# Attention over a KV cache on one core: four kv heads to a unit instead of two

## The chip, the cores and the metric

One core of one Trainium2 chip. The metric is the device time of one execution in microseconds (us); times of several executions are given as their median. Some executions are over 1.5% above the fastest of the same kernel and are called slow; comparisons use the others, the fast ones. A profiled execution gives a span, which is some 1.8 us shorter than the execution's time.

The terms: PE is the engine of the matrix products, DVE and ACT are those of element-wise work and copies. HBM is the chip's main memory, SBUF the core's working memory, PSUM the memory that takes PE's results. A load *lands* when its last bytes and its semaphore have arrived. The *granted clock* is the share of PE's full clock that PE was given.

## The reference

```python
B, Sq, D = 8, 4, 512;  Hq, Hkv, Sk, Dh = 32, 8, 2048, 128      # all bf16
q = (x @ wq) as [B, Hq, Sq, Dh]
scores = q . k * Dh**-0.5        # each of the 8 kv heads serves 4 query heads
o = softmax(scores) . v
out = o as [B, Sq, Hq*Dh] @ wo   # [8, 4, 512]
```

K and V are 33.6 MB each, wq and wo 4.2 MB each: 75.5 MB have to be read from HBM.

## The kernel before

It works through 32 units of two kv heads of one batch. A unit's K (1 MiB) lies on 128 partitions in rows of 8 KiB. PE transposes K (as pairs of bf16 in fp32) into PSUM, DVE copies that to SBUF, PE makes scores from it, ACT takes their exponentials, PE transposes the probabilities, ACT copies them to SBUF (block by block, between zeros), and PE multiplies them with V. The units are interleaved by hand; each engine runs its instructions in the order of this program.

```python
KB, VB = 7, 6                                   # K and V buffers of 1 MiB
def load_k(u):
    ...
    nc.sync.dma_start(ks[u][:, :, :],
        k_cache[b, 2*p : 2*p + 2].rearrange("g (s c) d -> (g s) c d", c=C))

def scores(u):
    s_ps = psum_s.tile([128, JT, 2, 64], FP32, tag="s", name="s_ps")   # 2 KiB
    for g in range(2):
        for e in range(2):
            for t in range(4):
                nc.tensor.matmul(s_ps[t*32:(t+1)*32, :, g, :], lhsT=q_bd[...],
                                 rhs=kt[(u, t)][:, :, g*64:(g+1)*64, e], ...)
    ...
    for g in range(2):                          # after the matmuls of both
        nc.scalar.activation(out=s_sb[:, :, g, :], in_=s_ps[:, :, g, :], func=EXP, ...)

def probs_to_keys(u):
    ...                                         # 4 transposes of 128x128 into pt
    for g in range(2):
        rows = slice(g*64, (g+1)*64)
        nc.scalar.copy(out=pr[rows, :, g, :], in_=pt[rows, :, :]...)   # 64 x 512

for n in range(NU + A):                         # w = n - 2
    transpose_part(n, 0); transpose_part(n, 1)
    scores(n - 1)
    transpose_part(n, 2); transpose_part(n, 3)
    values(w); norms(w) if w % 2 == 0; finish(w)     # guards cut
    probs_to_keys(n - 1)
    load_ready(...)                             # issues loads whose buffer comes free
```

The first 480 rows of wo go to SBUF in eight loads of five partitions each, the rest of wo in loads of 128 partitions.

The softmax here doesn't subtract the row's maximum and nothing guards it: scores larger than these inputs give would overflow.

## Time and profile before

| | before |
|---|---|
| time, median of 3 | 191.22 us (189.67 to 192.31) |
| span of the profiled execution | 188.2 us |
| busy: PE, DVE, ACT | 149.1, 109.0, 69.4 us |
| mean granted clock of PE | 0.945 |
| read from HBM | 75.5 MB |

The prediction below shows the views that carry the argument.

### The profile page before, as it was taken

To read this page: it belongs to the slowest core of one execution; us is meant where nothing else is said; L and a number is where in the kernel's file an instruction comes from. 1 tells how busy PE (TensorE), PEld (TensorE's weight loads), DVE (VectorE), ACT (ScalarE), POOL (GpSimd) and SP (SyncE) were. 2 spreads that over 40 slices of the span, in tenths; PEclk is the share of its full clock that TensorE was granted. 3 is DMA by queue.
4 is the path that set the end of the run, shared out by engine and by line. 5 is a ranking of instruction groups with operands and counts; after the bars stand their busy time and mean duration, and the time that the engine had idled before them with its cause. 6 is when DMAs were issued, how large, how long until landed. Compare 5 with 4: busy or idle time off the path is not lost.

```text
span 188.2 us, 5654 instructions
## 1 busy us (share of the span) xinstructions
PE 149.1 (79%) x2483; PEld 123.5 (66%) x2483; DVE 109.0 (58%) x217; ACT 69.4 (37%) x202; POOL 6.3 (3%) x9
## 2 busy tenths in 40 slices
PE   0535799978788788899999988787799888888493
PEld 0515488857676567788877767676588677667372
DVE  0580598765467577447876756657376767663220
ACT  2001574461343334144455352524245433436200
POOL 8400000000000000000000000000000000000000
PEclk9999999999699999858999999999699999999958
DMA  6999999999999999999999999999999999999960
GB/s 212 456 446 383 426 432 417 428 428 429 417 427 423 425 421 434 420 421 432 427 416 428 430 416 428 427 421 421 428 423 423 428 421 423 427 427 413 384 239 8
DMA packets 10952, 75.92 MB, mean 403 GB/s; under 512 B 1288, under 2 KB 1416, under 8 KB 2568
## 3 DMA queue, kind: packets, MB, share of 16 engines
q1 hardware_dynamic: 10880, 75.55, 96.0%
q8 instruction: 19, 0.31, 0.6%
q14 instruction: 5, 0.04, 0.1%
q10 hardware_dynamic: 48, 0.02, 0.0%
HBM read 75.53 MB, written 0.03 MB: 402 GB/s over the span
## 4 chain that ended last, share of the span: by engine, by line
DMA 76%; PE 17%; DVE 2%; issue 1%; ACT 1%; SPq 0%
DMA k_sb<-in_k_cache_dram 50%; DMA v_sb<-in_v_cache_dram 10%; DMA wo_m<-in_wo_dram 9%; DMA x_sb<-in_x_dram 7%; PE kp L198 6%; PE out_ps L397 3%; PE s_ps L261 2%; PE psq L220 2%; DVE kt L200 1%; PE o_ps L321 1%; PE l_ps L303 1%; DVE q_bd L245 1%; PE pt L280 1%; PE nat L345 0%; PE pse L236 0%
## 5 line engine op out<-in xcount | busy, mean ns | idle before, releaser
L200 DVE COPY kt<-kp 128x1024 bf16<-128x1024 bf16 x128 | 82.7, 686 | 38.5 <-PE kp L198 38.5
L198 PE MATMUL kp<-ident,k_sb 128*128 128x128 f32 x512 | 74.6, 293 | 22.6 <-DMA k_sb<-in_k_cache_dram 13.4
L198 PEld LDWEIGHTS kp<-ident,k_sb 128*128 128x128 f32 x512 | 59.7, 149 | 34.4 <-issue 16.2
L286 ACT COPY probs<-pt 64x512 bf16<-64x512 bf16 x64 | 37.1, 579 | 54.2 <-PE pt L280 53.8
L272 ACT ACTIVATE s_sb<-s_ps 128x256 bf16<-128x256 f32 x64 | 23.9, 379 | 33.4 <-PE s_ps L261 19.5
L321 PE MATMUL o_ps<-probs,v_sb 128*128 128x32 bf16 x1024 | 30.7, 177 | 1.2 <-ACT probs L286 0.7
L321 PEld LDWEIGHTS <-v_sb 128*128 128x128 bf16 x1024 | 30.0, 96 | 2.4 <-DMA v_sb<-in_v_cache_dram 1.7
L261 PE MATMUL s_ps<-kt,q_bd 128*32 128x256 bf16 x512 | 21.7, 291 | 0.0
L261 PEld LDWEIGHTS <-q_bd 128*32 128x32 bf16 x512 | 10.9, 97 | 6.7 <-issue 5.7
L311 DVE RECIPROCAL r_sb<-l_ps 128x64 f32<-128x64 f32 x16 | 8.9, 558 | 8.8 <-PE l_ps L303 8.8
L272 ACT ACTIVATION_READ_ACCUMULATOR s_sb<-s_ps 128x1 f32 x64 | 12.7, 198 | 0.0
L280 PE MATMUL pt<-ident,s_sb 128*128 128x128 bf16 x128 | 12.6, 221 | 0.0
L303 PE MATMUL l_ps<-by_gq,ones 128*128 128x64 f32 x32 | 7.2, 307 | 5.5 <-DVE by_gq L296 5.5
L303 PEld LDWEIGHTS l_ps<-by_gq,ones 128*128 128x128 f32 x32 | 5.0, 195 | 7.1 <-DVE by_gq L296 5.3
L280 PEld LDWEIGHTS <-s_sb 128*128 128x128 bf16 x128 | 9.1, 106 | 0.2 <-ACT s_sb L272 0.2
L332 DVE TENSOR_TENSOR oT<-o_ps,r_sb 128x32 bf16<-128x32 f32 x32 | 6.1, 191 | 4.7 <-PE o_ps L321 4.0
L227 ACT ACTIVATE qT_all<-psq 128x256 bf16<-128x256 f32 x4 | 1.5, 383 | 16.8 <-PE psq L220 16.8
L397 PE MATMUL out_ps<-wo_sb,oP 128*32 128x256 bf16 x48 | 5.5, 404 | 0.0
L245 DVE CAST q_bd<-pse 64x512 bf16<-64x512 f32 x4 | 2.6, 681 | 4.6 <-PE pse L236 4.6
L173 POOL MEMSET wo_e<- 64x6144 bf16 x1 | 5.2, 5211 | 0.3 <-POOLq L470 0.3
L296 DVE TENSOR_TENSOR by_gq<-l_sb,by_q 128x64 f32<-128x64 f32 x16 | 3.4, 215 | 2.1 <-ACT s_sb L272 2.1
L397 PEld LDWEIGHTS <-oP 128*32 128x32 bf16 x48 | 3.7, 142 | 1.1
(45 smaller groups left out, 38.0 us busy)
## 6 DMA issues: line engine op xcount, KB each, us to landing
k_sb<-in_k_cache_dram SPq DMA_DIRECT2D x32, 1024.0 KB, 19.6
v_sb<-in_v_cache_dram SPq DMA_DIRECT2D x32, 1024.0 KB, 13.1
wq_sb<-in_wq_dram SPq DMA_DIRECT2D x1, 4096.0 KB
wo_sb<-in_wo_dram SPq DMA_DIRECT2D x4, 512.0 KB
wo_sb<-in_wo_dram SPq DMA_DIRECT2D x4, 256.0 KB, 7.9
wo_m<-in_wo_dram SPq DMA_DIRECT2D x1, 512.0 KB
wo_e<-in_wo_dram SPq DMA_DIRECT2D x8, 60.0 KB
x_sb<-in_x_dram SPq DMA_DIRECT2D x1, 32.0 KB, 14.1
```

Source lines behind the costliest of these rows:

```text
L173: nc.gpsimd.memset(wo_e[:, :, :], 0.0)
L198: nc.tensor.transpose(kp[:, j, :], k4[:, w : w + 128], ident4[:, :])
L200: nc.vector.tensor_copy(out=k_t[:, :, :, :].rearrange("k j s e -> k (j s e)"), in_=kp[:, :, :].rearrange("k j s -> k (j s)").bitcast(BF16),)
L261: nc.tensor.matmul(s_ps[t * 32 : (t + 1) * 32, :, g, :], lhsT=q_bd[:, p, e, b, g, :, :], rhs=kt[(u, t)][:, :, g * 64 : (g + 1) * 64, e], s ...
L272: nc.scalar.activation(out=s_sb[:, :, g, :], in_=s_ps[:, :, g, :], func=EXP, accum_out=l_sbs[u][:, u % 2, g : g + 1])
L280: nc.tensor.transpose(pt[:, j, :], s_sbs[u][:, j, :, :].rearrange("q g s -> q (g s)"), ident[:, :])
L286: nc.scalar.copy(out=pr[rows, :, g, :], in_=pt[rows, :, :].rearrange("s j (c q) -> s (j c) q", q=HQ),)
L303: nc.tensor.matmul(l_ps[:, :, :].rearrange("d u q -> d (u q)"), lhsT=ones[:, :], rhs=by_gq[:, :, :, :].rearrange("k u g q -> k (u g q)"), ...
L311: nc.vector.reciprocal(r_sb[:, :, :], l_ps[:, :, :])
L321: nc.tensor.matmul(o_ps[:, :], lhsT=vs[u][:, 2 * (t * JT + j) + c, :], rhs=pr[:, i, :, :].rearrange("s g q -> s (g q)"), start=(i == 0), s ...
L332: nc.vector.tensor_tensor(out=oT[(p + 1) // 2][:, :, (p == 2) * 1, b, :], in0=o_pss[u][:, :].rearrange("d (h s) -> d h s", h=HP), in1=r_sb ...
L397: nc.tensor.matmul(out_ps[half * T : (half + 1) * T, :], lhsT=o, rhs=w[:, half * DH : (half + 1) * DH], start=(p == 0 and r == 0), stop=(p ...
```

## The change

The intent: K and V in units of four heads, so that each row on a partition is 16 KiB and each transfer 2 MiB; fewer, longer packets for the same bytes. There are then 16 units, 3 + 3 buffers of 2 MiB, and 320 wo rows go through five engines. The compute is rearranged to fit. The core of the diff:

```diff
-    KB = 7
-    VB = 6
+    KB = 3
+    VB = 3
-    NE, WE, WM = 40, 12, 4
+    NE, WE, WM, WN = 40, 8, 5, 64
-            k_cache[b, 2 * p : 2 * p + 2].rearrange("g (s c) d -> (g s) c d", c=C),
+        rows = cache[b, 4 * p : 4 * p + 4].rearrange("g (s c) d -> (g s) c d", c=C)
 ...                                                    (ktpool 6 -> 5, psum_s 1 -> 2)
-        s_ps = psum_s.tile([128, JT, 2, 64], FP32, tag="s", name="s_ps")
-        for g in range(2):
+        for g2 in range(2):
+            s_ps = psum_s.tile([128, 2, JT, 32], FP32, tag="s", name="s_ps")
+            for g1 in range(2):
+                g = 2 * g2 + g1
 ...                                                    (the 8 matmuls of group g)
-        for g in range(2):
-            nc.scalar.activation(
-                out=s_sb[:, :, g, :], in_=s_ps[:, :, g, :], func=EXP, ...
+                nc.scalar.activation(
+                    out=s_sb[:, :, g, :], in_=s_ps[:, g1, :, :], func=EXP, ...
 ...
-        for g in range(2):
-            rows = slice(g * 64, (g + 1) * 64)
+        for g in range(4):
+            rows = slice(g * 32, (g + 1) * 32)
             nc.scalar.copy(                             (64 x 512 -> 32 x 1024)
 ...
-        for t in range(2):
-            if 0 < n < NU:
-                transpose_part(n, t)
+        if 0 < n < NU:
+            transpose_part(n, 0)
         if 0 <= n - 1 < NU:
             scores(n - 1)
-        for t in range(2, 4):
+        for t in range(1, 4):
 ...                                                    (norms each unit; ends cut)
```

## The prediction

> **What bounds the kernel now.** I read the page's slices first, then the busy time by stretch, then the DMA queue's own waits, then the chain and the timeline of the end. The slices (one digit or number for each fortieth of the span, 4.7 us):
>
> ```profile
> PE   0535799978788788899999988787799888888493
> DMA  6999999999999999999999999999999999999960
> GB/s 212 456 446 383 426 432 417 428 428 429 417 427 423 425 421 434 420 421 432 427 416 428 430 416 428 427 421 421 428 423 423 428 421 423 427 427 413 384 239 8
> ```
>
> The 16 DMA engines are busy in every slice from the second to the last but two, at one rate, while PE has gaps everywhere. The busy time by stretch (start:end; then PE, PE weight load, DVE, ACT, POOL busy us; granted clock, DMA share, GB/s) gives the rate in the middle and its fall at the end:
>
> ```profile
> 80.00:100.00 20.00, 19.43 (x304) 16.53 (x308) 13.81 (x27) 9.15 (x26) 0.00 (x0) 0.86 1.01 424
> 100.00:120.00 20.00, 17.87 (x316) 14.51 (x305) 13.06 (x26) 8.50 (x27) 0.00 (x0) 1.00 1.01 424
> ...
> 178.00:180.00 2.00, 1.72 (x25) 1.47 (x21) 0.60 (x2) 0.00 (x0) 0.00 (x0) 0.50 0.88 343
> 180.00:181.00 1.00, 1.00 (x13) 0.63 (x12) 0.27 (x1) 0.00 (x0) 0.00 (x0) 0.50 0.83 326
> 181.00:182.00 1.00, 1.00 (x13) 0.71 (x14) 0.29 (x1) 0.00 (x0) 0.00 (x0) 0.50 0.57 217
> 182.00:183.00 1.00, 1.00 (x12) 0.76 (x10) 0.00 (x0) 0.00 (x0) 0.00 (x0) 0.50 0.37 143
> ```
>
> In the middle: share 1.01 and 424 GB/s, nothing idle. From 178 us the engines run dry one after another. The DMA queue's own waits show that it is held back by transfers still in flight, hardly by compute freeing a buffer:
>
> ```profile
> SPq L123 <- DMA v_sb<-in_v_cache_dram: 47.4, 22, 2.9
> SPq L113 <- DMA k_sb<-in_k_cache_dram: 44.2, 22, 2.2
> ...
> SPq L123 <- PE kp L198: 4.7, 15, 0.4
> ```
>
> The last stretch of the chain of waits (start, us, what) shows how the end hangs on the last landings:
>
> ```profile
> 160.13 16.31 DMA wo_m<-in_wo_dram
> 176.44 0.04 issue
> 176.48 0.82 PE out_ps L397 x10
> 177.31 0.94 PE o_ps L321 x32
> ...
> 181.01 4.11 PE out_ps L397 x40
> 185.13 0.02 issue
> 185.15 0.37 ACT out_sb L453
> ```
>
> So the time is: a start of 2.4 us until bytes flow, a solid stream of 75.5 MB, and some 9 us of dependent work after wo_m lands at 176.48, which runs beside the last 3 MiB of wo.
>
> **One packet.** The trace's record of DMA packets (start, duration, size) has median durations of 84 ns for 2 KiB, 159 for 4 KiB, 309 for 8 KiB, 460 for 12 KiB and 1213 for 32 KiB (the rows of wq). They lie on a line: (1213 - 309) / 24,576 B = 36.8 ps per byte, which is 435 GB/s on 16 engines, plus 8 ns. On one engine the next packet starts 3 ns before the last one ends, so an 8 KiB packet takes 306 ns of an engine, and a semaphore packet (9 ns) takes 6. The fixed part is therefore only some 5 ns in 306.
>
> **What the Trainium skill says.**
> "DMA: Bandwidth & Descriptors", section "Bandwidth", measures 341 GB/s for one transfer of 1 MB and 425 for 16 MB and advises large transfers. That is for a transfer by itself. This trace has 1 MiB transfers at 424 GB/s, since up to eight are queued: the fixed cost is already hidden, and 2 MiB can't win it again.
> The same page, "Why small descriptors are slow (HBM only)", gives a fixed cost of about 3 cycles per packet. The trace agrees that there is a small fixed part: 5 ns in 306.
> The same page, "Why a DMA increments its semaphore by 16 and not by 1", says that a load of 5 partitions uses 5 engines, the lowest-numbered ones. The trace agrees on the count: 1,256 semaphore packets before the output are 76 loads of 16 and 8 wo_e loads of 5.
> "TensorE: Matmul & The Clock Gate", Part 1, says that PE falls to half its clock after an idle window of some 3.4 us. The trace agrees: after the thin stretch from 172 to 176.5 us the granted clock is 0.50 from 178 us on.
>
> **The change, part by part.**
>
> *Runs of 16 KiB, transfers of 2 MiB.* By the line, a 16 KiB packet takes 309 + 8192 x 0.0368 = 610 ns, 607 of an engine's time. An engine's part of 2 MiB was 16 x 306 + 2 x 6 = 4908 ns and becomes 8 x 607.3 + 6 = 4864: 44 ns less. Of the 32 transfers, the first K and the last V are cut in two and keep runs of 8 KiB, so 30 x 44 ns = **1.3 us** on the path. The whole sum over all packets says the same: (8192 x 306 + the rest) / 16 = 177.0 us before, 175.7 after.
>
> *320 rows instead of 480 through five engines.* In the packet record the engines end at different times: about eight near 181.15 us, eight between 182.0 and 183.66. Joining packets end to start, imperfectly, the five tracks with most of the wo_e packets end at 182.0 to 183.66, so they seem overloaded. The other late ones probably took more of the 19 instruction fetches of 16 KiB (0.93 us each), which the five extra loads are meant to balance. A wo_e packet becomes 8 KiB, so each of the five has 8 x 151 ns = 1.2 us less, and every engine gets 160 KiB / 16 = 10 KiB = 0.37 us more. The five end 0.8 us sooner, the rest 0.4 later; the last engine ends perhaps 0.2 us sooner. I take **-0.2** (between +0.3 and -0.8).
>
> *Compute for four heads.* The built order shows the same 512 K transposes, 128 K copies on DVE, 512 score matmuls, 64 exponentials, 128 probability transposes, 1024 value matmuls. Two things grow. The 64 ACT copies of probabilities go from 512 to 1024 elements: 579 ns, plus 512 x 0.8 ns (from 383 ns at 256 elements and 590 at 512), about 990; so ACT goes from 69 to some 95 us. The value matmuls have 64 columns instead of 32. Both are beside the stream: in the catch-up stage of the chain, two old units (one new) take 7.7 us (28.91 to 36.61), against 2 x 4.9 = 9.8 us of loading. With wider values and six K groups in a row waiting for DVE (686 ns a copy against about 440 of PE) I put a new unit at 8.4 to 8.7 us. On the path: 0.
>
> *Start.* x now comes behind 2 MiB of K instead of 1, so it lands 2.4 us later, at about 18. The queue holds some 40 us of loads that need nothing from this; DMA doesn't stop. On the path: 0.
>
> *End.* 3 MiB of wo still follow the last landing that matters, now the second half of the last V. The 5 to 6 last rows of project(0) leave the chain (-0.8), but the norms of the last unit enter it (a matmul 0.43, reciprocal 0.56: +1.0), one more multiply (+0.2), wider value matmuls and transposes (+0.4). With PE at half clock that is +0.8 us. If PE stays warm, because project(0) and half the values now fill the gap ahead of it, the 40 last matmuls take half of their 4.1 us and the end follows the last wo landing: -0.6 us. I take **+0.1**.
>
> Sum: -1.3 - 0.2 + 0.1 = -1.4 us, so 191.22 becomes **189.8 us**.
>
> **The rivals.**
> *Buffers starve the stream.* 7 + 6 buffers of 1 MiB become 3 + 3 of 2 MiB, and a transfer is issued only once a whole 2 MiB has been read. For it: the queue's waits on DMA will turn into waits on PE. Against: K(u+3) needs K(u) read, about 6 us after it landed, and is due on the engines only some 24 us after; V has 20 us. PE would have to lag by 18 us. If it did, by 5 us at the start say, the time would be 194 to 196.
> *Large transfers win much more.* If 1 MiB transfers lost something between them, doubling would save several us. Against: share 1.01 and gaps of -3 ns between packets. The ceiling of the line, 435 against 427 GB/s, is worth at most 3.3 us even without any fixed cost; with the tail warm and the engines even (slowest 1.7 us above the mean) it would make 187.
> *Compute becomes the bound.* PE or ACT over 9.7 us a unit would show as a DMA share below 1. At ACT 6.3 us (4 x 0.58 + 4 x 0.99) and PE 8.7 it isn't near; if wrong by 15%, 16 units would add about 4 us.
> *16 KiB rows are slower to read.* The 32 KiB rows of wq fit the line exactly, so I give this little.
>
> **Range and chances.** Runs of before spread from 189.67 to 192.31 us, so a median of three moves by about 1 us; tail and balance add 1 us either way. Range 188.0 to 191.4. Faster by over 2% means under 187.4, which needs even engines, a warm tail and luck: 0.11. Slower by over 2% needs starvation: 0.03.
>
> **What would show it.** Right: 16 KiB packets near 610 ns; 429 to 430 GB/s in the middle and DMA share still 1.0; the queue's waits on PE, yet no dip; ACT copies near 990 ns; x at about 18 us; a smaller spread of the engines' ends. The half clock or full clock in the last 6 us decides the tail. Wrong: slices under 9 in DMA (starvation), packets well off 610 ns, or last landings that spread more than before.

## More of the kernel before

The columns of a group are line, engine, operation, out and in with shapes and count; then busy us and mean ns of one; then the idle time of the engine just before, and what ended it:

```profile
L286 ACT COPY probs<-pt 64x512 bf16<-64x512 bf16 x64 | 37.1, 579 | 54.2 <-PE pt L280 53.8
...
L261 PE MATMUL s_ps<-kt,q_bd 128*32 128x256 bf16 x512 | 21.7, 291 | 0.0
```

What to see: the last figure of the score matmuls is 0.0. PE never stands idle ahead of them. ACT is the engine that waits.

## The result

| | before | after |
|---|---|---|
| median of 4 | 190.96 us | 260.69 us |
| span of the profiled execution | 188.2 us | 258.5 us |
| busy: PE, DVE, ACT | 149.1, 109.0, 69.4 us | 173.6, 112.1, 99.0 us |
| mean granted clock of PE | 0.945 | 0.815 |

The ratio is 1.364 (95% interval 1.352 to 1.375). A ratio here is the mean time of one kernel's fast runs over that of the other's of the same rounds, so not quite the ratio of the medians. The change made the kernel 36% slower; the prediction was within 1% of no change.

The slices of the changed kernel (6.5 us each):

```profile
PE   0377739486685939393949485884957849392955
...
PEclk9997995959595898679786979597795968677799
DMA  7999999999979595959695968778393291991000
GB/s 262 468 412 427 418 440 435 415 435 407 423 260 422 171 441 183 426 175 413 226 388 226 370 281 332 319 274 375 86 425 145 63 375 26 360 395 39 3 3 5
```

For the first eleven slices, some 70 us, the stream is as solid as before. Then DMA goes on and off, slice by slice, and so does PE; no engine is busy all the time. The two groups, in the columns explained above:

```profile
L282 ACT COPY probs<-pt 32x1024 bf16<-32x1024 bf16 x64 | 64.2, 1003 | 106.3 <-PE pt L276 105.1
...
L260 PE MATMUL s_ps<-kt,q_bd 128*32 128x256 bf16 x512 | 30.1, 343 | 63.9 <-ACT s_sb L267 63.9
```

The copies take 1003 ns (the prediction had 990). But PE is now idle for 63.9 us ahead of the score matmuls, and what it waits for is the exponential on ACT. The view of waits, longest first, adds how often (engine and line, what ended the wait, us in total, times, longest):

```profile
ACT probs L282 <- PE pt L276: 105.1, 16, 10.9
...
PE s_ps L260 <- ACT s_sb L267: 63.9, 32, 4.4
```

There are 32 of them, two in each of the 16 units; the kernel before has no such row. ACT in turn waits for PE's probability transposes once a unit. The DMA queue's own waits have turned too:

```profile
SPq L113 <- PE kp L194: 133.4, 12, 12.9
SPq L113 <- PE l_ps L299: 45.4, 11, 17.6
...
SPq L113 <- DMA k_sb<-in_k_cache_dram: 3.6, 1, 3.6
```

The queue stands for 133 us because PE has not yet read a K buffer. Whether that is cause or consequence, the profile does not say; the experiments do.

One turn, as the timeline shows it (start, us, engine, line and operation, count; idle before it and what ended it):

```profile
102.14 0.61 PE L276 MATMUL pt<-ident,s_sb 128*128 128x128 bf16 x8
...
102.84 4.09 ACT L282 COPY probs<-pt 32x1024 bf16<-32x1024 bf16 x4 [6.56 <-PE pt L276]
...
103.56 0.40 PE L260 MATMUL s_ps<-kt,q_bd 128*32 128x256 bf16 x8
106.95 0.38 ACT L267 ACTIVATE s_sb<-s_ps 128x256 bf16<-128x256 f32 x1
...
107.48 1.05 PE L260 MATMUL s_ps<-kt,q_bd 128*32 128x256 bf16 x16 [3.51 <-ACT s_sb L267]
```

Eight score matmuls (group 0) run at 103.56. Those of group 1 wait until 107.48, because the exponential of group 0 starts only at 106.95: it stands on ACT behind the four probability copies of the previous unit. PE does not go past the waiting matmul, so the 24 K transposes that come next wait too.

Why must group 1 wait for group 0's exponential? They touch different halves of one tile. The tile has 2 x 8 x 32 fp32 numbers on a partition, 2 KiB. The Trainium skill, "PSUM — Partial Sum Buffer", gives that as the size of a bank ("Terms") and, in the section "PSUM bank collisions raise a hardware error", says that a PE write and an ACT read in one bank and the same 32 partitions are an error even at disjoint columns, and that they have to be kept apart by semaphores per bank and quadrant (those 32 partitions), not per address. The trace agrees: in each unit the first matmul of group 1 and the first of group 3 carry a wait for the semaphore of ACT's exponentials, 32 in all, and no other score matmul does. The two groups share the tile as well as the bank, so no run here tells which of the two the wait is kept by. With the exponentials after both groups, as before, there is nothing to wait for.

The chain of waits goes through the whole turn without a gap (start, us, what; of the four copies one line is shown):

```profile
109.71 4.29 PE kp L194 x24
114.00 1.86 PE o_ps L318 x64
...
116.12 0.46 PE pt L276 x8
...
116.66 1.01 ACT probs L282
...
120.77 0.48 ACT s_sb L267 x2
...
121.30 0.45 PE s_ps L260 x6
...
121.77 0.85 ACT s_sb L267 x4
...
122.66 0.42 PE s_ps L260 x7
```

From 109.71 to the next turn's start at 123.08 it is 13.4 us: PE 4.3 + 1.9 + 0.3 + 0.5, ACT 4.1 + 0.5, PE 0.45, ACT 0.85, PE 0.4. The loads of a unit take 9.7 us (two transfers of 4.86, by the prediction's sum). By the starts of the reciprocals in the trace (one a unit, from 46.8 to 250.1 us), the mean turn is (250.1 - 46.8) / 15 = 13.55 us.

### The profile page after: what moved, and what is told of

Its sections match the earlier page's. It is cut to its first block, busy times and chain, and to the rows that moved or that the text cites. A ratio compares the mean times of both kernels' runs of the same rounds, so it can differ in the third digit from the quotient of the medians.

```text
span 258.5 us, 5542 instructions
## 1 busy us (share of the span) xinstructions
PE 173.6 (67%) x2465; PEld 151.6 (59%) x2466; DVE 112.1 (43%) x216; ACT 99.0 (38%) x202; POOL 4.7 (2%) x9
## 4 chain that ended last, share of the span: by engine, by line
PE 52%; ACT 34%; DMA 6%; DVE 3%; issue 2%; SPq 0%; ACTq 0%
PE kp L194 25%; ACT probs L282 25%; PE o_ps L318 11%; ACT s_sb L267 8%; PE s_ps L260 7%; DMA x_sb<-in_x_dram 6%; PE pt L276 3%; PE l_ps L299 2%; PE psq L215 2%; DVE kt L195 1%; PE out_ps L393 1%; DVE q_bd L240 1%; DVE nat_sb L346 1%; PE perm L360 1%; ACT q_bd L240 0%
## 5 line engine op out<-in xcount | busy, mean ns | idle before, releaser
L282 ACT COPY probs<-pt 32x1024 bf16<-32x1024 bf16 x64 | 64.2, 1003 | 106.3 <-PE pt L276 105.1
L194 PE MATMUL kp<-ident,k_sb 128*128 128x128 f32 x512 | 91.0, 353 | 10.0 <-DMA k_sb<-in_k_cache_dram 6.0
L194 PEld LDWEIGHTS kp<-ident,k_sb 128*128 128x128 f32 x512 | 83.2, 189 | 17.7 <-issue 6.8
L260 PE MATMUL s_ps<-kt,q_bd 128*32 128x256 bf16 x512 | 30.1, 343 | 63.9 <-ACT s_sb L267 63.9
L260 PEld LDWEIGHTS <-q_bd 128*32 128x32 bf16 x512 | 14.5, 107 | 75.3 <-issue 73.9
L318 PE MATMUL o_ps<-probs,v_sb 128*128 128x64 bf16 x1024 | 34.0, 196 | 2.4 <-ACT probs L282 2.4
L318 PEld LDWEIGHTS <-v_sb 128*128 128x128 bf16 x1024 | 33.5, 100 | 3.2 <-issue 2.8
L179 DVE MEMSET probs<- 128x2048 uint32 x2 | 3.5, 1765 | 0.8 <-issue 0.8
L215 PE MATMUL psq<-xT_sb,wq_sb 128*128 128x32 bf16 x128 | 3.5, 182 | 0.3 <-DVE xT_sb L208 0.3
L215 PEld LDWEIGHTS <-wq_sb 128*128 128x128 bf16 x128 | 3.5, 100 | 0.3 <-issue 0.3
```

The lines of the kernel that those rows point to most:

```text
L194: nc.tensor.transpose(kp[:, j, :], k4[:, w : w + 128], ident4[:, :])
L215: nc.tensor.matmul(psq[:, h, :], lhsT=wq_sb[:, r, hh * 128 : (hh + 1) * 128], rhs=xT_sb[:, r, :], start=(r == 0), stop=(r == R - 1),)
L260: nc.tensor.matmul(s_ps[t * 32 : (t + 1) * 32, g1, :, :], lhsT=q_bd[:, 2 * p + g2, e, b, g1, :, :], rhs=kt[(u, t)][:, :, g * 32 : (g + 1) ...
L282: nc.scalar.copy(out=pr[rows, :, g, :], in_=pt[rows, :, :].rearrange("s j (c q) -> s (j c) q", q=HQ),)
L318: nc.tensor.matmul(o_ps[:, :], lhsT=vs[u][:, 2 * (t * JT + j) + c, :], rhs=pr[:, j * 8 + t * 2 + c, :, :].rearrange("s g q -> s (g q)"), s ...
```

## The experiments

All kernels of this section computed the right result, except e2. The kernel before, run beside them, had a median of 189.41 us beside e1 to e4 and of 190.5 beside e5 to e12; each ratio is to those runs. The last landing is the last semaphore packet of the last wo load in the trace.

| run | median us | ratio (95%) | last landing, us |
|---|---|---|---|
| e1 exponentials after both groups | 194.50 | 1.023 (1.015 to 1.030) | 181.8 |
| e2 half-width copies, waits kept | 221.47 | 1.153 (1.142 to 1.164) | - |
| e3 before, exponentials interleaved | 191.17 | 1.005 (0.998 to 1.012) | - |
| e4 e1, K order of before | 193.55 | 1.019 (1.012 to 1.025) | 183.6 |
| e5 e1, end reordered | 187.44 | 0.985 (0.982 to 0.988) | 182.1 |
| e6 e5, last norms first | 187.49 | 0.986 (0.983 to 0.989) | 181.9 |
| e7 e6 with runs of 8 KiB | 190.01 | 0.997 (0.993 to 1.001) | 183.5 |
| e8 e6 with 480 rows | 188.54 | 0.992 (0.988 to 0.996) | 182.1 |
| e9 e6, buffers 128 bytes lower | 189.11 | 0.993 (0.989 to 0.997) | 183.7 |
| e10 e6, K order of before | 188.24 | 0.991 (0.986 to 0.996) | 184.6 |
| e11 before, each copy twice | 191.16 | 1.002 (0.996 to 1.007) | - |
| e12 before, interleaved and copies twice | 230.64 | 1.210 (1.204 to 1.216) | - |

**e1, the wait taken away.** The theory: the wait above. The rivals: buffers too few and too coarse, or ACT's longer work.

```diff
         for g1 in range(2):
             ...                        # the 8 matmuls of group g
-            nc.scalar.activation(out=s_sb[:, :, g, :], in_=s_ps[:, g1, :, :], ...)
+        for g1 in range(2):
+            g = 2 * g2 + g1
+            nc.scalar.activation(out=s_sb[:, :, g, :], in_=s_ps[:, g1, :, :], ...)
```

> The changed kernel with one edit: the exponentials of a pair of groups come after the score matmuls of both, not between them. Theory (the wait): the score matmuls of groups 1 and 3 wait for the exponential of groups 0 and 2, which stands behind four probability copies of 4.1 us on ACT, so PE and ACT take turns for 13.7 us a unit. Without that wait PE alone has about 0.9 + 1.7 + 4.4 + 1.9 + 0.25 + 0.5 = 9.7 us a unit, about as long as the loads (9.7 us): 189 to 197 us, no wait of score matmuls for ACT. Rival 1 (buffers too few and too coarse): nothing changes there, so over 245 us. Rival 2 (ACT's copies, twice as long, are too much work): ACT has the same work, so over 245 us.

194.5 us: 66 us came back from moving one loop. The row of score matmuls waiting for ACT is gone. In the timeline:

```profile
100.82 3.29 PE L194 MATMUL kp<-ident,k_sb 128*128 128x128 f32 x24
...
106.76 4.08 ACT L284 COPY probs<-pt 32x1024 bf16<-32x1024 bf16 x4 [4.09 <-PE pt L278]
...
109.47 1.13 PE L260 MATMUL s_ps<-kt,q_bd 128*32 128x256 bf16 x32
```

All 32 score matmuls of the next unit run in one piece at 109.47, while ACT is still in the copies it began at 106.76. The mean turn by the reciprocals is (183.2 - 38.1) / 15 = 9.67 us, the time of the loads. That accounts for the spans: 15 turns x (13.55 - 9.67) = 58.2 us, the first reciprocal 8.7 us sooner, the end 1.5 us longer: 65.4 us, which is 258.5 - 193.1. Buffers and ACT's work are the same in e1, so both rivals fall as causes of the 66 us. Nor are the queue's waits for a K buffer the cause: of the 133 us, 51.8 (12 times) are still there in e1, where DMA is busy throughout the middle (428 to 430 GB/s from 40 to 160 us), and the rest went with the wait.

The 24 K transposes take 3.29 us here, against 4.36 in the timeline of the changed kernel. The Trainium skill, "TensorE: Matmul & The Clock Gate", Part 1, explains such a difference by the clock that falls when PE pauses. The traces agree: in the changed kernel, after a pause of 3.51 us, the granted clock was 0.50 from 107.4 to 109.6 us and 0.64 over the transposes (109.6 to 114.0); in e1 it was 1.00 over them. The means of the two executions are 0.815 and 0.912. So the wait cost twice: in itself, and in a slower PE after it. No run splits the 66 us between the two.

**e2, a dose of the chain.**

```diff
-                out=pr[rows, :, g, :],
-                in_=pt[rows, :, :].rearrange("s j (c q) -> s (j c) q", q=HQ),
+                out=pr[rows, : C // 2, g, :],
+                in_=pt[rows, : JT // 2, :].rearrange("s j (c q) -> s (j c) q", q=HQ),
```

> The changed kernel with the probability copies cut to half their columns (result wrong on purpose: half of the probabilities stay zero); the interleaved exponentials stay. Theory (the wait): the copies lie in the chain of every unit, so 4 x (1.00 - 0.59) = 1.65 us a unit goes, for about 15 units 25 us: 233 to 239 us. Rival 1 (buffers): under 3 us of change. Rival 2 (ACT is the bound by its work): also shorter by about 25 us, so this run does not tell it from the theory; e1 does.

219.0 us as the mean of the two fast runs of four (relative error 0.65, as intended). The sign is right, the size is not: 42 us less than the changed kernel, not 25. In the profiled execution, a slow one, the copies took 576 ns, as expected, so 1.7 us a unit are the copies themselves; the mean turn fell by 2.1 us, to 11.4, and the granted clock of the fast runs rose to 0.906 and 0.913 from 0.815. The rest fits a PE that pauses less and so slows less, but this run does not isolate that.

**e3, e11 and e12, the parts alone, in the kernel before.** Is interleaving bad in itself, or only with the longer copies? e3 interleaves the two exponentials of the kernel before, e11 does each of its copies twice, e12 does both.

```diff
 e3:      for g in range(2):
              ...                           # the 8 matmuls of group g
+             nc.scalar.activation(out=s_sb[:, :, g, :], in_=s_ps[:, :, g, :], ...)
-         for g in range(2):
-             nc.scalar.activation(...)
 e11: -        for g in range(2):           # in probs_to_keys
      +        for g in (0, 0, 1, 1):
```

> The kernel before, with only the exponentials put between the score matmuls of its two groups, as the change does. Theory (the wait, and what stands behind it): the same wait arises, but only two copies of 0.58 us stand ahead of the exponential, and the turn-taking chain of a unit of two heads is 1.2 (copies) + 0.5 + 0.35 + 1.0 + 0.95 + 0.2 + 0.25 + gaps = about 4.6 us against 4.9 us of loads: 190 to 197 us. Rival 3 (the interleaving by itself is fatal, whatever the copies take): over 220 us.

> The kernel before with each probability copy done twice on ACT (result unchanged), exponentials not interleaved. ACT's work rises from 69 to 106 us of 188. Theory (long copies hurt only where a wait of PE stands behind them): up to 2% slower, 189 to 194 us. Rival 2 (ACT's longer work itself costs the time): clearly slower, over 205 us.

> The kernel before with both: exponentials interleaved and copies done twice. Theory (the two together): the chain of a unit of two heads grows from 4.6 by 1.2 us to about 5.8 us, over the 4.9 us of loads, and PE's clock falls in the gaps: 32 units x 5.8 to 6.3 us + start and end = 215 to 240 us, though e3 and e11 each stay near 190. Rival (the coarse units and buffers of the changed kernel are needed for the loss): near 190 to 195.

Ratios 1.005, 1.002 and 1.210: either one alone costs nothing that these rounds resolve, both together cost 21%. The waits of the score matmuls in e3 and in e12:

```profile
PE s_ps L264 <- ACT s_sb L271: 21.0, 32, 1.4
```

```profile
PE s_ps L264 <- ACT s_sb L271: 51.0, 32, 2.6
```

In e3 the 32 waits are there, 0.7 us each, and PE has that much to spare in 4.9 us of loads. (The profiled run of e3 was a slow one.) In e12 they are 1.6 us each and the turn no longer fits. ACT was busy 106.7 us in e11 without harm. So the loss needs neither large units nor few buffers. It takes both the wait and long work on ACT in front of what PE waits for.

**e4, the K transposes as before (two parts ahead of the scores, two after), on top of e1.** It needed one more buffer for transposed K (kt), and an unused tile 128 bytes smaller to make room.

> As e1, and K transposes two parts ahead of the scores and two after them as in the kernel before (one more kt buffer, an unused pad made smaller). Theory: DVE's six copies in a row no longer hold PE back, PE's unit falls to about 8.7 us, the loads bound again, and the prediction's own 189 to 190.5 us should be seen, with the middle at 429 to 430 GB/s. Rival 1 (buffers): over 245 us. If e1 is already bound by the loads, e4 equals e1.

193.55 us: within the spread of e1, and not the 189 to 190.5 expected. This was the second miss: with the wait gone, the kernel was still 2% slower than before, though in e1 the stream ended at 181.8 us, 1.8 sooner than in the kernel before. So some 11.3 us passed after the last landing instead of 4.5. The end of e1 shows why:

```profile
165.98 4.08 ACT L284 COPY probs<-pt 32x1024 bf16<-32x1024 bf16 x4 [4.00 <-PE pt L278]
...
170.11 3.57 PE L320 MATMUL o_ps<-probs,v_sb 128*128 128x64 bf16 x64 [3.19 <-ACT probs L284]
...
175.11 4.08 ACT L284 COPY probs<-pt 32x1024 bf16<-32x1024 bf16 x4 [3.46 <-PE pt L278]
...
179.24 3.57 PE L320 MATMUL o_ps<-probs,v_sb 128*128 128x64 bf16 x64 [0.90 <-ACT probs L284]
```

The last two units go one after the other: copies, values, copies, values. There is no next unit to fill the gaps. The copies of the last unit end at 179.2, some 5 us after its V landed (174.1). PE was also slow here: the granted clock was 0.50 from 169.2 to 182.8 us, and the value matmuls of a unit took 3.57 us, against 1.86 in the chain above.

**e5 and e6, the end reordered.**

```diff
 e5:  for t in range(1, 4):
+         if n == NU - 1 and t == 3:
+             probs_to_keys(n - 1)          # unit 14's, before the last K part
          if 0 < n < NU:
              transpose_part(n, t)
+     if n == NU:
+         probs_to_keys(n - 1)              # unit 15's, before unit 14's values
      ...
-     if 0 <= n - 1 < NU:
+     if 0 <= n - 1 < NU - 2:
          probs_to_keys(n - 1)
 e6: + if w == NU - 1: norms(w)             # before values(w) in the last unit
```

> e1 with the probability transposes of the last two units moved ahead: unit 14's before the last K part of unit 15, unit 15's right after its scores, both before the value matmuls they stood behind. Theory (the rest of the loss is at the end): in e1 the stream ends 1.8 us sooner than in the kernel before (181.8 against 183.7), but the last two units run one after the other through 4.1 us of copies each, so the end comes 11.3 us after the last landing instead of 4.5. Reordered, the copies of unit 15 end near 173 instead of 179.2, ahead of the last V, and the time falls by 5 to 6 us to 188 to 190. Rival (the loss of 4 us in e1 is in the middle, from PE being as long as the loads): it stays at 193 to 195.

> e5 with the last unit's norms ahead of its value matmuls, since they need only its scores. Theory: a matmul of 0.43 and a reciprocal of 0.56 us leave the chain after the last V: 0.6 to 1 us less than e5, 187 to 189.3 us, 0.3 to 1.2% under the kernel before. If the end hangs on the last wo landing instead: equal to e5.

187.44 and 187.49 us. e5 took 7 us off e1; the rest of the loss was at the end. Part of the 7 us is PE's clock, which was 1.00 from 166 to 182 us in e5. e6 equals e5, and its chain says why:

```profile
155.87 18.88 DMA v_sb<-in_v_cache_dram
...
174.76 7.45 DMA wo_sb<-in_wo_dram
...
182.26 0.41 PE out_ps L395 x4
```

The end now hangs on the last wo landing, with four matmuls behind it, so 0.6 to 1 us of compute saved ahead of it buys nothing. e5 is 1.5% faster than the kernel before, clear of noise though under 2%: the version that beats both.

**e7 and e8, the two terms of the prediction's sum, each undone in e6.**

```diff
 e7: -        ks[u] = load(kpool, "k_sb", k_cache, u, 2 if u == 0 else 1)
     +        ks[u] = load(kpool, "k_sb", k_cache, u, 2)           # V likewise
 e8: -    NE, WE, WM, WN = 40, 8, 5, 64
     +    NE, WE, WM, WN = 40, 12, 4, 32           # and an unused tile 128 bytes smaller
```

> e6 with each K and V load cut in two loads of 1 MiB with runs of 8 KiB, all else equal: measures the one term of the prediction that the intent rests on. Prediction's own term: 30 x 44 ns = 1.3 us, so last landing and time 1.3 us later than e6 (188.3 to 190.6), 309 ns packets. Rival (large transfers matter much more than packets show): over 4 us slower than e6.

> e6 with the 480 wo rows through five engines of the kernel before instead of 320. Prediction's own term: the five engines get 0.8 us more, the others 0.4 less; the last landing 0.2 us later on average, spread of the 16 ends larger (1.7 instead of about 1.5 us): time within 0.5 us of e6.

e7: runs of 8 KiB cost 2.1 us (mean of fast runs 189.68 against 187.61), and the last landing comes 1.6 us later (183.5 against 181.9). The middle of the stream, 40 to 140 us, ran at 422.7 against 426.7 GB/s. So the longer packets and larger transfers together are worth 1.6 to 2.1 us. e8: 480 rows cost 1.1 us (188.71 against 187.61), though the last landing is only 0.2 us later and the 16 KiB packets stay at 611 ns. In that profile PE ends 1.3 us later for another reason: the last unit's probability transposes start at 171.9 instead of 169.9 us. What made PE late there stays open.

**e9 and e10, the confounder of e4.** In e4 the 16 KiB packets took 613 ns in the median, not 611, and the stream ended 1.7 us later than e1's. The 128 bytes by which a tile was made smaller were suspected.

```diff
 e9:  -    pad = const.tile([128, 96], BF16, name="pad")
      +    pad = const.tile([128, 32], BF16, name="pad")
 e10: e6 with two K parts ahead of the scores and two after; pad0 256 bytes smaller
```

> e6 with an unused tile 128 bytes smaller, so that all buffers after it lie 128 bytes lower in SBUF. e4, where the same edit was made to gain room, had 16 KiB packets of 613 to 614 ns instead of 611 and a last landing at 183.6 instead of 181.8. If the place of the buffers does it: 613 to 614 ns here too, and 0.7 to 1.7 us slower than e6 (188.2 to 189.2). If not: 611 ns and e6's time.

> e6 with K transposed two parts ahead of the scores and two after (e4's order), room gained by 256 bytes instead of 128. The loads bind in the middle already (426.7 GB/s), so the order should be worth nothing: within 0.5 us of e6, 611 ns packets. If PE's unit of 9.7 us still costs something in e6: 1 us faster or more.

e9: 613 ns again, last landing 183.7 against 181.9, 1.5 us slower than e6. The place of the buffers in SBUF does it, whatever the mechanism. e10, with a shift of 256 bytes, has 611 ns, and 188.24 us: its four runs lie between 187.63 and 190.17, and the profiled one was the slowest. The K order buys nothing; its median is 0.75 us above e6, a little outside the 0.5 us expected, which is too near to e10's own spread to read more into.

## Why the prediction was wrong

It failed at the part "Compute for four heads", which ends "I put a new unit at 8.4 to 8.7 us. On the path: 0." A new unit took 13.55 us. The durations in that step were right: ACT copies 1003 ns against 990, ACT busy 99.0 us against 95. What was missing is the order. The step summed each engine's work by itself, and the rival "Compute becomes the bound" was dismissed by the same sums (PE 8.7, ACT 6.3, both under 9.7). But PE and ACT did not run side by side: the exponential inside the loop makes the score matmuls of the same PSUM bank wait for ACT, ACT reaches that exponential only after 4.1 us of copies, and PE in its program order stands still meanwhile. e1 shows this by removing the wait alone, e12 by producing it in the kernel before. The diff showed the moved loop, and the built program carries the two waits in each unit; the prediction counted instructions and did not read what they wait for. It also cites no page for the moved access to a PSUM tile. Its rival put the cost, if the sums were 15% off, at about 4 us; moving one loop gave back 66.

Step by step:

- *One packet.* Right. 16 KiB packets took 611 ns in the median, predicted 610.
- *The stream's gain, 1.3 us.* Right in mechanism, somewhat small: 1.6 us in landings, 2.1 in time (e7).
- *320 rows, 0.2 us.* In landings 0.2, in time 1.1 (e8); the difference is not explained.
- *Start, 0.* The x load took 16.3 us from issue to landing, against 14.1 before, as predicted. Nothing in e5 suggests that it cost time, but no run isolates it.
- *End, +0.1.* Wrong, and a term of its own: e5 against e1 shows 7 us. The chain was started at the landing of the last V; in fact it started at the copies of the last two units, whose doubled length matters where no other unit is left to fill in. The working priced copies only in the middle. Its citation on the half clock is also a little more than its trace shows: ahead of the 0.50 at 178 us PE's longest pause was 2.15 us, so the kernel before shows the fall, but not the page's 3.4 us.
- *The rival of buffers.* The queue's waits did turn to PE, as said, and the stream did starve, so this rival and its sign (DMA slices under 9) looked right in the profile. e1 has the same six buffers and a solid stream. Starvation was the result of a late PE.
- *The rival of large gains.* Right to reject: 2 MiB and 16 KiB together are worth 1.6 to 2.1 us.
- *The rival of slow 16 KiB rows.* Right to reject, by the 611 ns. The reason given was no test: the line was drawn through the 32 KiB rows themselves. The 2, 4 and 12 KiB packets lie on it too, and they do test it.

With the wait and the end mended, e5 comes to 187.44 us beside 190.5: 1.5% faster. The prediction's gain of 1.4 us was near that of the data path, but e5 is a different kernel from the one that was predicted, with its end reordered too, so its gain is no support for the prediction.

## What to carry to other kernels

Before calling added work hidden because each engine's sum fits, walk one turn of the loop along the waits: an instruction moved inside a loop can make two engines take turns, and the cost is then everything that stands in the queue ahead of it. In these programs a write of PE and a read of ACT in one PSUM tile of a bank's size were a wait, even at different addresses; finish all writes to such a tile, then read it. And when units get larger, look at the last two by themselves: what the next unit hides in the middle is bare at the end.

## What the Trainium skill lacked or had wrong

- "PSUM — Partial Sum Buffer" has the rule, but not its price: that a wait for a bank includes whatever the other engine has queued first. Here that was 63.9 us in 32 waits, and 66 us of time.
- "DMA: Bandwidth & Descriptors", section "Bandwidth": it has 341 GB/s for a load of 1 MB issued from GpSimd, and no figure for loads in a queue. Queued loads of 1 MiB in 8 KiB rows ran at 422.7 GB/s here, and loads of 2 MiB in 16 KiB rows at 426.7 (e7 and e6, packets of the load queue, 40 to 140 us). The page has no figure for what rows of 8, 16 and 32 KiB cost a load to SBUF; here they took 309, 611 and 1213 ns of one engine.
- No page that we read has the effect of e9: the buffers 128 bytes lower in SBUF made 16 KiB packets 613 instead of 611 ns, moved the last landing by 1.7 us and cost 1.5 us of time. The DMA page's section "How a descriptor splits into AXI transactions" speaks of 256-byte alignment for reads only.
- "Perfetto Trace Analysis", section "Optimization Strategy", names one possible cause for a gap that repeats: too little SBUF or PSUM for the next tile. Here the repeated gap, 63.9 us in 32 waits, came from the place of an instruction in a loop, and it went with the same buffers (e1).
